# Who issues 32 stores: from SyncE's DMA queue to ScalarE's

## The chip, the cores and the metric

The kernel runs on one core of one Trainium2 chip. TensorE (PE) multiplies matrices, VectorE (DVE), ScalarE (ACT) and GpSimd (POOL) work elementwise, SyncE (SP) computes nothing and issues the DMA transfers. The metric is device time in microseconds (us) for one execution; the figure for a kernel is the median of its runs. Beside the runs one execution was recorded by the hardware profiler; its page and its trace are the source of every other number.

## The reference

The inputs are `x` (8 batches, 8 heads, 512 tokens, 64 features) and `state` (8, 8, 32, 64). For each batch and head two attentions are computed, and their results stand behind each other along the tokens:

```
scores = scale * x @ state^T;   xread = softmax(scores) @ state     # 512 rows
scores2 = scale * state @ x^T;  sread = softmax(scores2) @ x        # 32 rows
```

The heads are joined to rows of 512 features (8 x 544 rows), and a feed-forward layer with a rational function follows, with `w_in` 512 x 2048 and `w_out` 2048 x 512 given in 64-bit floating point:

```
h = rows @ w_in
P = a0 + a1*h + a2*h^2 + a3*h^3
Q = 1 + |b0|*|h| + |b1|*h^2
out = (P / (Q + 1e-6)) @ w_out
```

## The kernel before, in words

The kernel never forms xread. Since xread @ w_in = softmax @ (state @ w_in), it computes the product of state and w_in once for each batch, called m here, and multiplies the transposed attention weights with it. The work of the feed-forward layer is cut into steps n = 8 * batch + u, where u counts eight slices of 256 columns of w_in; eight more steps at the end (n = 64 to 71) handle the sread rows of all batches.

**The order.** Every engine executes its instructions in program order. That order is written out by hand in `ORDER` as a list of tokens; the loop at the end of `attention_rational_ffn` calls one function for each token under a manual schedule. An instruction waits for the semaphores of what it depends on, and whatever stands behind it on the same engine waits too. This holds for SP's queue as well: a DMA whose data isn't ready holds back the DMAs behind it.

**The early stage** (to about 145 us) does these things at once:

- The 64-bit weights are loaded into `raw` tiles (L277 for w_in, L285 for w_out) and turned into 32-bit values: one ACT instruction (`conv_parts`, L300) and several on DVE (`join_rest` L309, `join_low` L321, `join_sign` L332). A finished slice of w_in is used at once and is also stored to HBM (L336). The w_out slices are split into a high and a low part by ACT (L342) and POOL (L343).
- Token `X:i` (`extra`, L626): PE multiplies the states of two batches with slice u of w_in, for all eight slices and four pairs of batches, so 32 times. The result fills a PSUM tile `ps_x` from the pool `ps_h`, tag `h`; this tag has two buffers, which the `h` tiles of the steps and several attention tiles share.
- Token `XA:i` (`extra_out`): ACT copies the tile from PSUM to an SBUF tile `xo` (L638; two buffers), and a DMA stores it to `m32` in HBM (L639). For the pair with batches 0 and 1 only batch 1 is copied and stored (8 stores of 256 KB); the other 24 are of 512 KB. Batch 0's part is used directly from PSUM (`fold_hi0`, L650 on ACT, and `fold_lo0`, L654 on DVE).
- Attention and the steps of batch 0 run beside this.

**A step** consists of the matmuls `F` (L705, into `h`), then on ACT the two functions C (L717) and A (L724), on DVE the products (L728, L732, L738), on ACT the absolute value (L744), logarithm and exponential for the reciprocal (L811, L821), on DVE L749, L755, L761, on POOL L768, and then the matmuls with w_out (L777), which accumulate into PSUM tiles `o`.

**The late stage** (from about 145 us) is these steps for the other batches. Their m is loaded back from `m32` (`load_m`, L660) into tiles that share the `raw` buffers, and split by ACT (L665) and POOL (L666).

All DMAs of the kernel are issued by SP: loads of the raw weights, of xT (L366) and x (L374) for the attention, the stores of w_in (L336) and of m (L639), the reloads of m (L660) and w_in (L349), and the stores of the output (L801, L804).

Of the kernel before, what the change touches and what calls it, by code (L numbers as in the profile page):

```python
# [186 lines left out]
def attention_rational_ffn(  # L187
# [6 lines left out]
    nc = tc.nc  # L194
# [439 lines left out]
    def extra_out(i, copy):  # L634
        u, e = divmod(i, B // 2)
        q0 = 1 if e == 0 else 0
        t = ew.tile([P, 2, 2, CW], F32, name="xo", tag="xo", bufs=2)
        copy(t[:, :, q0:], XP[i][:, :, q0:])  # L638
        nc.sync.dma_start(  # L639
            m32[2 * e + q0 : 2 * e + 2, u].rearrange("q p j f -> p j q f"),  # L640
            t[:, :, q0:],
        )
# [188 lines left out]
    def keep_warm(k):  # L831
# [38 lines left out]
        "lw": load_win,  # L870
        "X": extra,
        "XA": lambda i: extra_out(i, nc.scalar.copy),
        "XV": lambda i: extra_out(i, nc.vector.tensor_copy),
        "lm": load_m,
        "ls": load_state,
# [61 lines left out]
```

## Time and profile before

| | value |
|---|---|
| median of 3 runs | 718.27 us |
| lowest and highest of them | 716.25 and 720.06 us |
| profiled execution: its own time | 720.89 us |
| profiled execution: span from first to last instruction | 719.1 us |
| granted TensorE clock, mean over the span | 0.981 |
| PE busy | 676.1 us (94%) |
| DVE busy | 646.1 us (90%) |
| ACT busy | 516.5 us (72%) |
| POOL busy | 309.0 us (43%) |

The profiled execution lies 2.6 us above the median of the runs. Busy times count computing instructions; issuing a DMA is not counted as busy. In the trace an instruction named SPq is one of SP's sequencer, so a DMA issue. For a DMA the trace has two times: how long the issuing instruction took, and how long after its start the data had landed. The number in brackets behind a line of the timeline is the idle time of the engine before it, with what ended it.

### The profile page before, as it was taken

To read this page: it belongs to the slowest core of one execution; us is meant where nothing else is said; L and a number is where in the kernel's file an instruction comes from. 1 tells how busy PE (TensorE), PEld (TensorE's weight loads), DVE (VectorE), ACT (ScalarE), POOL (GpSimd) and SP (SyncE) were. 2 spreads that over 40 slices of the span, in tenths; PEclk is the share of its full clock that TensorE was granted. 3 is DMA by queue.
4 is the path that set the end of the run, shared out by engine and by line. 5 is a ranking of instruction groups with operands and counts; after the bars stand their busy time and mean duration, and the time that the engine had idled before them with its cause. 6 is when DMAs were issued, how large, how long until landed. Compare 5 with 4: busy or idle time off the path is not lost.

```text
span 719.1 us, 11605 instructions
## 1 busy us (share of the span) xinstructions
PE 676.1 (94%) x4602; PEld 527.7 (73%) x4602; DVE 646.1 (90%) x605; ACT 516.5 (72%) x641; POOL 309.0 (43%) x172
## 2 busy tenths in 40 slices
PE   4578889999999999999999999999999999999994
PEld 3345555677877787778787878787877788888883
DVE  2789998999998999999899999998999889898894
ACT  2678878887777877677587767677787768855752
POOL 0012335385445553463444453535434545534550
PEclk8979999999999999999999999999999999999998
DMA  7988978824030402050313140223041102101201
GB/s 220 318 318 297 342 264 291 269 87 162 16 102 30 147 16 69 35 171 20 103 59 108 40 148 15 61 101 117 1 162 45 59 13 82 38 1 59 89 1 58
DMA packets 47874, 81.49 MB, mean 113 GB/s; under 512 B 3276, under 2 KB 25932, under 8 KB 47820
## 3 DMA queue, kind: packets, MB, share of 16 engines
q1 hardware_dynamic: 47820, 80.75, 33.3%
q8 instruction: 36, 0.59, 0.3%
q14 instruction: 18, 0.15, 0.1%
HBM read 52.95 MB, written 27.79 MB: 112 GB/s over the span
## 4 chain that ended last, share of the span: by engine, by line
PE 74%; DVE 12%; ACT 5%; DMA 4%; issue 2%; POOL 1%; SPq 0%; ACTq 0%; DVEq 0%; POOLq 0%
PE h L705 24%; DMA m_dram<-xo 3%; PE ps_x L626 3%; DVE C L728 2%; DVE A L738 2%; DVE gh L749 2%; PE o__1880 L777 2%; PE o__1823 L777 2%; PE o__3047 L777 2%; DVE C L732 2%; PE o__1899 L777 2%; PE o__3096 L777 2%; PE o__5489 L777 2%; PE o__5507 L777 2%; PE o__5463 L777 2%
## 5 line engine op out<-in xcount | busy, mean ns | idle before, releaser
L768 POOL TENSOR_TENSOR gl<-C,L 128x1024 fp32r<-128x1024 f32 (+1 forms) x71 | 173.8, 2448 | 271.0 <-DVE C L761 209.4
L705 PE MATMUL h<-aT,m 128*128 128x512 f32 x768 | 193.8, 398 | 4.8 <-ACT xo L638 3.7
L705 PEld LDWEIGHTS h<-aT,m 128*128 128x128 f32 x768 | 145.2, 191 | 40.4 <-ACT xo L638 5.1
L749 DVE SCALAR_TENSOR_TENSOR gh<-C,cst,L 128x1024 fp32r<-128x1024 f32 (+1 forms) x72 | 98.7, 1370 | 22.1 <-ACT L L821 3.0
L717 ACT ACTIVATE C<-h,cst 128x1024 f32<-128x1024 f32 (+1 forms) x72 | 83.0, 1155 | 46.7 <-PE h L705 26.2
L666 POOL TENSOR_TENSOR m<-m_sb,m 128x512 fp32r<-128x512 f32 x56 | 82.3, 1473 | 61.5 <-ACT m L665 42.9
L724 ACT ACTIVATE A<-h,cst 128x1024 f32<-128x1024 f32 (+1 forms) x72 | 76.5, 1064 | 44.4 <-PE h L705 41.3
L744 ACT ACTIVATE A<-A 128x1024 f32<-128x1024 f32 (+1 forms) x72 | 72.7, 1012 | 34.2 <-DVE A L738 34.2
L761 DVE SCALAR_TENSOR_TENSOR C<-C,cst,A 128x1024 f32<-128x1024 f32 (+1 forms) x72 | 93.2, 1294 | 1.7
L738 DVE SCALAR_TENSOR_TENSOR A<-A,b0a,h 128x1024 f32<-128x1024 f32 (+1 forms) x72 | 87.1, 1211 | 6.0 <-ACT C L717 5.6
L728 DVE TENSOR_TENSOR C<-C,h 128x1024 f32<-128x1024 f32 (+1 forms) x72 | 83.0, 1154 | 8.1 <-ACT C L717 6.1
L755 DVE SCALAR_TENSOR_TENSOR A<-A,gh 128x1024 f32<-128x1024 f32 (+1 forms) x72 | 88.4, 1228 | 1.6
L732 DVE SCALAR_TENSOR_TENSOR C<-C,cst,h 128x1024 f32<-128x1024 f32 (+1 forms) x72 | 87.8, 1220 | 1.9
L811 ACT ACTIVATE L<-A 128x1024 f32<-128x1024 f32 (+1 forms) x72 | 72.9, 1014 | 8.7 <-POOL gl L768 7.2
L821 ACT ACTIVATE L<-L 128x1024 f32<-128x1024 f32 (+1 forms) x72 | 72.9, 1012 | 0.9
L626 PE MATMUL ps_x<-win_sb,st 64*32 64x256 f32 x1024 | 38.5, 419 | 16.0 <-ACT xo L638 4.9
L343 POOL TENSOR_TENSOR wo<-cv_r,wo 128x512 fp32r<-128x512 f32 x16 | 22.1, 1401 | 61.9 <-ACT wo L342 61.9
L626 PEld LDWEIGHTS ps_x<-win_sb,st 64*32 64x32 f32 x1024 | 18.5, 114 | 31.4 <-ACT xo L638 8.7
L638 ACT COPY xo<-ps_x 128x1024 f32<-128x1024 f32 (+1 forms) x32 | 28.8, 906 | 9.2 <-DMA m_dram<-xo 5.5
L665 ACT CAST m<-m_sb 128x512 fp32r<-128x512 f32 x56 | 33.9, 612 | 1.3 <-PE h L705 1.2
L300 ACT ACTIVATE cv_y<-raw 128x512 f32<-128x512 f32 x32 | 21.3, 685 | 8.0 <-DMA raw<-in_w_in_dram 7.6
L705 PEld LDWEIGHTS h<-sh,m 128*128 128x128 f32 x192 | 24.3, 191 | 1.1 <-issue 0.3
(267 smaller groups left out, 1161.1 us busy)
## 6 DMA issues: line engine op xcount, KB each, us to landing
m_sb<-m_dram SPq DMA_DIRECT2D x56, 256.0 KB, 4.4
m_dram<-xo SPq DMA_DIRECT2D x24, 512.0 KB, 4.4
out_dram<-o_sb SPq DMA_DIRECT2D x34, 256.0 KB, 2.2
xT_sb<-in_xT_dram SPq DMA_DIRECT2D x16, 512.0 KB, 3.9
raw<-in_w_in_dram SPq DMA_DIRECT2D x16, 512.0 KB, 6.1
x_sb<-in_x_dram SPq DMA_DIRECT2D x16, 512.0 KB, 6.0
raw<-in_w_out_dram SPq DMA_DIRECT2D x16, 512.0 KB, 6.4
w_in_dram<-win_sb SPq DMA_DIRECT2D x8, 512.0 KB, 6.4
```

Source lines behind the costliest of these rows:

```text
L626: nc.tensor.matmul(ps[k * NS : (k + 1) * NS, j, q, :], st[j * D : (j + 1) * D, 2 * e + q, k, :], win_t[u][j * D : (j + 1) * D, k, :], star ...
L666: nc.gpsimd.tensor_tensor(m[:, 1], t, m[:, 0].bitcast(F32), op=ALU.subtract)
L705: nc.tensor.matmul(h[:, ci * W : (ci + 1) * W], l, r, start=(q == 0), stop=(q == len(seq) - 1),)
L717: nc.scalar.activation(e["C"], e["h"], AF.Identity, scale=cst[:, 3:4], bias=cst[:, 2:3])
L728: nc.vector.tensor_tensor(e["C"], e["C"], e["h"], op=ALU.mult)
L732: nc.vector.scalar_tensor_tensor(e["C"], e["C"], cst[:, 1:2], e["h"], op0=ALU.add, op1=ALU.mult)
L738: nc.vector.scalar_tensor_tensor(e["A"], e["A"], b0a, e["h"], op0=ALU.add, op1=ALU.mult)
L749: nc.vector.scalar_tensor_tensor(e["gh"], e["C"], cst[:, 0:1], e["L"], op0=ALU.add, op1=ALU.mult)
L755: nc.vector.scalar_tensor_tensor(e["A"], e["A"], 1.0 + 1e-6, e["gh"].bitcast(F32), op0=ALU.add, op1=ALU.mult)
L761: nc.vector.scalar_tensor_tensor(e["C"], e["C"], cst[:, 0:1], e["A"], op0=ALU.add, op1=ALU.subtract)
L768: eng.tensor_tensor(e["gl"], e["C"], e["L"], op=ALU.mult)
L777: nc.tensor.matmul(O[t], e[l][:, j * W + t * P : j * W + (t + 1) * P], wo[:, k, 2 * u + j, :], start=(u == 0 and l == "gh" and k == 0 and ...
```

## The change

The store of `xo` to `m32` is issued by ACT, the engine that has just made the copy, instead of SP. The 32 stores, their tiles, sizes and addresses stay the same, and so does the order of the tokens; no other DMA moves.

```diff
--- before.py
+++ after.py
@@ -636,7 +636,7 @@
         q0 = 1 if e == 0 else 0
         t = ew.tile([P, 2, 2, CW], F32, name="xo", tag="xo", bufs=2)
         copy(t[:, :, q0:], XP[i][:, :, q0:])
-        nc.sync.dma_start(
+        nc.scalar.dma_start(
             m32[2 * e + q0 : 2 * e + 2, u].rearrange("q p j f -> p j q f"),
             t[:, :, q0:],
         )
```

On SP the store was an instruction that waited for the copy's semaphore, with SP's later DMAs behind it. On ACT it is an instruction of ACT's sequencer that waits for the end of the copy on the same engine, with ACT's later instructions behind it.

## The prediction

> **What bounds the kernel now.** I read the stages first: where in the span the 32 stores lie, and which engine is full there. The rows are stretches of the span with the busy time of each engine; the cuts are mine: start-up, the stretch with the stores in three parts, and the rest.
>
> ```profile
> core 0: us, PE busy (x) PEld busy (x) DVE busy (x) ACT busy (x) POOL busy (x), PEclk, DMA share, GB/s
> 17.00:54.00 37.00, 24.27 (x366) 14.81 (x366) 30.67 (x47) 26.71 (x42) 2.53 (x2) 0.82 0.91 314
> 54.00:108.00 54.00, 45.84 (x588) 30.77 (x576) 53.35 (x55) 43.51 (x60) 16.68 (x9) 0.97 0.88 301
> 108.00:145.00 37.00, 35.57 (x490) 23.59 (x489) 33.49 (x38) 32.39 (x44) 17.48 (x10) 1.00 0.82 282
> 145.00:719.10 574.10, 562.32 (x3091) 452.25 (x3090) 524.37 (x462) 409.43 (x490) 271.63 (x146) 1.00 0.20 69
> ```
>
> From 145 us on PE is busy for 562.3 of 574.1 us: PE sets that time, and nothing in it is touched by the change. An early delay can't be won back there: PE has 11.8 us of idle left in the whole of it, and its matmuls follow in program order. So each microsecond by which PE leaves the first 145 us later is nearly a microsecond at the end.
>
> Between 17 and 145 us no engine is the bound alone. DVE is full in the middle (53.4 of 54 us), PE in the last part (35.6 of 37). ACT is busy for 26.7 + 43.5 + 32.4 = 102.6 of 128 us and idle for 25.4. How much of this idle time the stores cost or could take is the question. The next view is that of the tile: the copy, the DMA that stores it, who waited for the copy, and the time from issue to landing.
>
> ```profile
> L638 ACT COPY xo<-ps_x x32: 562/1012/1041, 17.3 to 141.1; 128x1024 f32<-128x1024 f32 x24, 128x512 f32<-128x512 f32 x8
> L639 SPq DMA_DIRECT2D m_dram<-xo x32: 522/585/1198, 18.1 to 142.1; - x32
>   PEld ps_x L626: 8.7, 10
>   PEld h L705: 5.1, 4
> DMA to landing us min/median/max: 2.6/4.5/9.8
> ```
>
> All 32 lie between 17 and 142 us. SP's sequencer spends 0.585 us on an issue (median; 0.522 to 1.198). PE's weight loads waited 14 times, 13.8 us in all, until such a copy had emptied a PSUM buffer: ACT's lateness reaches PE at once, for the two buffers leave no reserve. The last view is the waits between 17 and 145 us: first SP's, then the ACT and DVE waits that the DMAs end.
>
> ```profile
> SPq L639 <- ACT xo L638: 48.4, 19, 5.5
> SPq L639 <- ACT cv_y L300: 9.1, 5, 4.0
> ...
> ACT xo L638 <- DMA m_dram<-xo: 5.5, 6, 1.6
> ACT cv_y L300 <- DMA raw<-in_w_in_dram: 1.6, 2, 1.1
> ...
> DVE cv_r L309 <- DMA raw<-in_w_in_dram: 1.1, 2, 0.6
> ```
>
> SP stands for 57.5 us before stores whose copy isn't made yet. That looks like a great loss, but it is SP's time, and SP computes nothing. What it costs others is in the lower rows: loads of raw weights that came late held ACT for 1.6 us and DVE for 1.1, and a copy that wanted an `xo` buffer whose store hadn't landed held ACT for 5.5 us.
>
> **What the change removes.** From SP it takes 32 issues and 57.5 us of standing. Loads behind a store (L277, L285, L366, L374) can then go out earlier; the most that this can give is the 1.1 + 1.6 us of waits for raw weights. I take 0 for it: the two rows are 4 waits of 1.1 us at most, at the start of the stretch, and later loads wait for buffers that DVE frees. The reloads of m (L660) come late in it and read what was stored long before; POOL's queue is not passed. The transfers stay: the same bytes on the same DMA engines, which are 82 to 91% busy here.
>
> **What it adds.** On ACT, each of the 32 copies is followed by a wait for its own end and by an issue, and all of ACT's next instructions stand behind it. The price is put together from these rows of the timeline and of the chain:
>
> ```profile
> 55.37 9.42 DMA m_dram<-xo
> 64.82 0.04 issue
> 71.30 0.99 ACT L638 COPY xo<-ps_x 128x1024 f32<-128x1024 f32 x1
> 72.19 1.12 ACT L724 ACTIVATE A<-h,cst 128x1024 f32<-128x1024 f32 x1
> 72.32 0.58 SPq L639 DMA_DIRECT2D m_dram<-xo  x1
> ```
>
> Today the next activation starts at 72.19, which is 0.10 us before the copy ends at 72.29: consecutive ones overlap. This overlap goes (0.10). From the copy's end to SP's issue 0.03 us pass; the issue takes 0.585; from a released wait to the next instruction I take the chain's 0.04. Together 0.755 us for a large store; for the eight small ones I take the shortest issue, 0.522, and get 0.69. That is 24 * 0.755 + 8 * 0.69 = 23.6 us of ACT's time. No row shows an issue on ACT. The nearest row is the same transfer issued by SP, and I take that. The bounds are the longest issue of such a store, 1.198 us, and SP's shortest issue of any kind:
>
> ```profile
> 14.12 0.23 SPq L237 DMA_DIRECT2D cst<-in_cb_dram  x1
> ```
>
> With 0.23 us a store costs 0.40 us, 12.8 us in all; with 1.198 it costs 1.37, 44 us in all.
>
> The Trainium skill, page "DMA: Bandwidth & Descriptors", section "Issuing engines are not separate DMA queues", speaks against the change: whoever issues, the transfers share the 16 DMA engines, and issuing elsewhere saves only the sequencer's time for starting them. By that rule the gain is SP's 32 issues, which nobody waits for, and the sum stays what ACT pays.
>
> **How much of it reaches the end.** 23.6 us of new work against 25.4 us of idle time: by the total ACT could just hold it; by parts it can't. At 0.755 and 0.69 us, the 8 stores up to 54 us cost 5.8 us (idle 10.3), the 14 up to 108 us 10.4 (idle 10.5), the 10 after that 7.4 (idle 4.6, so 2.8 too much even if every gap were used). Gaps are used only where they lie. So I walked along the chain that ended last and looked, at each place where ACT stands on it, how many stores come before it and how much idle time lies between them. The rows are ACT's own, with the idle time in brackets, and three pieces of the chain (77.48, 82.47, 102.49):
>
> ```profile
> 28.40 1.93 ACT L638 COPY xo<-ps_x 128x1024 f32<-128x1024 f32 x2
> 33.77 1.01 ACT L638 COPY xo<-ps_x 128x1024 f32<-128x1024 f32 x1 [1.00 <-DMA m_dram<-xo]
> 51.78 0.59 ACT L638 COPY xo<-ps_x 128x512 f32<-128x512 f32 x1
> 58.00 0.62 ACT L638 COPY xo<-ps_x 128x512 f32<-128x512 f32 x1
> 64.86 1.01 ACT L638 COPY xo<-ps_x 128x1024 f32<-128x1024 f32 x1 [1.59 <-DMA m_dram<-xo]
> 67.17 1.02 ACT L638 COPY xo<-ps_x 128x1024 f32<-128x1024 f32 x1 [0.70 <-ACT cv_y L300]
> 69.01 0.27 ACT L585 COPY srT<-ps_sr__472 128x128 f32<-128x128 f32 x1 [0.82 <-PE ps_sr__472 L580]
> 75.31 1.03 ACT L638 COPY xo<-ps_x 128x1024 f32<-128x1024 f32 x1
> 77.48 0.56 ACT cv_y L300
> 82.47 0.70 ACT cv_y L300
> 101.26 0.56 ACT L638 COPY xo<-ps_x 128x512 f32<-128x512 f32 x1
> 101.72 0.58 ACT L650 CAST m<-ps_x 128x512 fp32r<-128x512 f32 x1
> 102.49 0.61 DVE m L654
> 119.09 0.58 ACT L638 COPY xo<-ps_x 128x512 f32<-128x512 f32 x1 [1.19 <-DMA m_dram<-xo]
> 121.10 2.18 ACT L638 COPY xo<-ps_x 128x1024 f32<-128x1024 f32 x2
> 134.86 1.93 ACT L638 COPY xo<-ps_x 128x1024 f32<-128x1024 f32 x2 [0.83 <-PE ps_x L626]
> 139.90 0.99 ACT L638 COPY xo<-ps_x 128x1024 f32<-128x1024 f32 x1
> 141.07 1.01 ACT L638 COPY xo<-ps_x 128x1024 f32<-128x1024 f32 x1 [0.17 <-PE ps_x L626]
> 142.14 1.02 ACT L536 CAST aT<-ps_a 128x1024 fp32r<-128x1024 f32 x1
> ```
>
> - At 33.77 two stores stand before the copy, 1.51 us, and a gap of 1.00 takes up most: +0.5.
> - At 64.86 three (after 51.78, 54.17 and 58.00), 2.14 us, gap 1.59: +0.55.
> - At 77.48 four (after 64.86, 67.17, 71.30, 75.31), 3.02 us, gaps 0.70 and 0.82: +1.5.
> - At 82.47 the store of the copy just ended comes in between, without a gap: +0.75.
> - At 102.49 DVE needs ACT's cast, which ends at 102.30; with the small store ahead of it 102.99: +0.5.
> - At 121.10 and behind it the small store and one large one, 1.45 us; the gap of 1.19 before them is used up by the two stores ahead of it: +1.4.
> - At 142.14 the stores after the two copies at 134.86 and the one at 139.90, 2.27 us, with 0.17 of gap: +2.1. Here PE, full until then, needs the PSUM buffer and the cast.
>
> The sum is +7.3 us. Elsewhere longer gaps lie behind the stores; I count nothing there. That cover is thin where ACT's gap is a wait for PE and PE in turn waits for ACT's copies: then the gap moves along with the delay and takes up nothing.
>
> Against the profiled execution this gives 720.9 + 7.3 = 728.2 us; that execution is 2.6 us above the median of the runs, so I forecast 718.3 + 7.3 = **725.6 us**. With the cheapest issue (0.40 us a store) the same walk gives 0, 0, 0.1, 0.4, 0.2, 0.4 and 1.0: +2.1 us, or 720.4. With twice the walk, that is, if a delay also eats the gaps behind it, it is +14.6, or 732.9. These two are the forecast's own range.
>
> **Rivals.** The first ends on the other side: *faster, because stores no longer stand in SP's line.* Today a store is queued behind loads that SP issued before it, and the landing spreads from 2.6 to 9.8 us; ACT's wait for it is 5.5 us. If on its own queue a store lands near the short end, this 5.5 goes, and with the raw loads' 2.7 at most 8.2 us are won. It decides if ACT's issue costs near the lower bound: then -5.5 + 2.1 = -3.4, or 714.9 us. For it speaks that the wait for a store stands in the walk at 33.77, 64.86 and 119.09; against it, that these gaps are the very ones that take up the issues in my sum, and that ACT is then free only to stand at the issue. The Trainium skill, page "DMA: Bandwidth & Descriptors", section "Queues, rings and completion order", supports this rival: a DMA engine alternates between the queue rows that have work. No run shows it yet; the only dynamic queue of this kernel is SP's.
>
> The second: *no change.* ACT's 25.4 us of idle time hold the 23.6 us, since PE's and DVE's waits are elastic at those places: 718.3 us. For it speaks the total; against it, the last 37 us, where ACT lacks 2.8 us, and DVE, which has 0.65 us of reserve in the middle.
>
> The third: *the whole price.* ACT becomes the bound, each gap moves along, and all 23.6 us show: 741.9 us. For it speak ACT's 54 us between 54 and 108, which would be full to 53.9; against it, the gaps up to 54 us, which wait for DVE and for raw loads and hold 5.8 us easily.
>
> That the change doesn't do what it says I rule out: one call names the issuing engine, and nothing else depends on it.
>
> **How the numbers follow.** The forecast gets 0.61, the whole price 0.11, no change 0.18, faster 0.10. A measurement here can tell about 0.5% from no change, 3.6 us. Of the forecast's 0.61, 0.06 lies under +3.6 us. So slower is 0.55 + 0.11 = 0.66, same 0.18 + 0.06 = 0.24, faster 0.10. The range goes from 716 us, into the faster case, to 737 us, beyond twice the walk; it leaves out part of the faster case and most of the whole price, under 2 in 10 together.
>
> **What would show it.** In the profile of the changed kernel, 32 issues at L639 should stand on ACT's queue at about 0.585 us, each followed by a gap of some 0.65 us before ACT's next instruction; SP's waits at L639 should be gone. PE's idle time between 17 and 145 us, now 22.3 us, should be some 7 us more, and the stretch behind it as long as before. The sum is wrong if ACT's instructions overlap the issue (no gap behind the copy), if an issue on ACT is far from 0.585 us, or if the late stretch changes length. The faster rival is right if ACT's wait for stores vanishes and landings shorten without PE's idle time growing.

## The result: slower by 2.7%, and the profile after

The median went from 717.8 us (of four runs; the table ahead of the prediction has three) to 739.0 us: the ratio is 1.0268, with a 95% interval of 1.023 to 1.0306, so 19.2 us over the kernel before by the ratio (21.2 between the medians). The direction was forecast, the size was not: the forecast was +7.3 us, and the range ended at 737. The profiled execution took 738.26 us, its span is 736.5, which is 17.4 more than the span of before; that pair is compared here.

The first view cuts each span at the same instruction, the start of PE's matmuls into `h` that stood at 142.1 us before (157.7 us after). The columns are those of the stretches in the prediction. The kernel before:

```profile
17.00:142.10 125.10, 102.81 (x1416) 66.85 (x1416) 115.26 (x136) 100.04 (x141) 33.80 (x20) 0.93 0.87 299
142.10:719.10 577.00, 565.19 (x3103) 454.56 (x3102) 526.62 (x464) 412.01 (x494) 274.53 (x147) 1.00 0.21 70
```

The changed kernel:

```profile
17.00:157.70 140.70, 106.60 (x1417) 68.63 (x1414) 114.52 (x135) 100.68 (x140) 35.56 (x20) 0.90 0.80 269
157.70:736.50 578.80, 566.41 (x3102) 455.71 (x3102) 527.12 (x463) 412.11 (x494) 271.92 (x147) 0.99 0.21 69
```

15.6 of the 17.4 us are lost in the early stretch, 1.8 behind it. In the early one PE's idle time grows from 125.1 - 102.8 = 22.3 to 140.7 - 106.6 = 34.1 us, so by 11.8; the other 3.8 us are PE's own: the same matmuls took longer at a granted clock of 0.90 instead of 0.93.

The next rows are the tile's in the changed kernel, with what its copies waited for, and the timeline of ACT around two copies:

```profile
L639 ACTq DMA_DIRECT2D m_dram<-xo x32: 530/587/612, 17.1 to 157.7; - x32
  DMA m_dram<-xo: 9.3, 6
DMA to landing us min/median/max: 3.3/4.9/10.8
```

```profile
27.70 1.01 ACT L638 COPY xo<-ps_x 128x1024 f32<-128x1024 f32 x1
28.74 0.59 ACTq L639 DMA_DIRECT2D m_dram<-xo  x1
31.31 1.01 ACT L638 COPY xo<-ps_x 128x1024 f32<-128x1024 f32 x1 [2.61 <-DMA m_dram<-xo]
32.35 0.59 ACTq L639 DMA_DIRECT2D m_dram<-xo  x1
32.98 0.59 ACT L536 CAST aT<-ps_a__295 128x512 fp32r<-128x512 f32 x1 [0.66 <-ACT xo L638]
```

The reader sees two losses. One is what was priced: the copy ends at 32.32, the issue starts 0.03 later, takes 0.59, and ACT's next instruction begins 0.66 us after the copy's end. The other wasn't in the sum: the copy at 31.31 first stands 2.61 us until a store has landed and freed its `xo` buffer. Before, ACT's copies stood 5.5 us for landings; now it is 9.3, and one more wait of 1.9 us that the view puts down to DVE belongs to it, so 11.2 us in all; for in the chain it is a landing that ends it:

```profile
88.64 10.67 DMA m_dram<-xo
99.35 0.04 issue
99.39 0.59 ACT xo L638
```

### The profile page after: what moved, and what is told of

The parts are those of the page before. It is cut to its first block, busy times and chain, and to the rows that moved or that the text cites. A ratio compares the mean times of both kernels' runs of the same rounds, so it can differ in the third digit from the quotient of the medians.

```text
span 736.5 us, 11591 instructions
## 1 busy us (share of the span) xinstructions
PE 681.1 (92%) x4602; PEld 530.9 (72%) x4602; DVE 646.6 (88%) x605; ACT 518.0 (70%) x641; POOL 308.2 (42%) x172
## 4 chain that ended last, share of the span: by engine, by line
PE 65%; DVE 14%; ACT 7%; DMA 7%; issue 3%; POOL 1%; ACTq 1%; SPq 0%; DVEq 0%; POOLq 0%
PE h L705 22%; DMA m_dram<-xo 5%; DVE gh L749 2%; ACT xo L638 2%; DVE C L728 2%; DVE A L738 2%; DVE C L761 2%; DVE A L755 2%; PE ps_x L626 2%; DVE C L732 2%; PE o__5489 L777 2%; PE o__5507 L777 2%; PE o__6031 L777 2%; PE o__4314 L777 2%; PE o__6046 L777 2%
## 5 line engine op out<-in xcount | busy, mean ns | idle before, releaser
L705 PE MATMUL h<-aT,m 128*128 128x512 f32 x768 | 196.0, 401 | 6.0 <-ACT xo L638 4.1
L705 PEld LDWEIGHTS h<-aT,m 128*128 128x128 f32 x768 | 146.8, 193 | 42.5 <-ACT xo L638 5.8
L666 POOL TENSOR_TENSOR m<-m_sb,m 128x512 fp32r<-128x512 f32 x56 | 80.8, 1447 | 62.4 <-ACT m L665 43.9
L626 PE MATMUL ps_x<-win_sb,st 64*32 64x256 f32 x1024 | 40.3, 435 | 24.6 <-ACT xo L638 12.5
L300 ACT ACTIVATE cv_y<-raw 128x512 f32<-128x512 f32 x32 | 21.2, 680 | 11.1 <-DMA raw<-in_w_in_dram 7.0
```

What stands on the lines that cost most here:

```text
L626: nc.tensor.matmul(ps[k * NS : (k + 1) * NS, j, q, :], st[j * D : (j + 1) * D, 2 * e + q, k, :], win_t[u][j * D : (j + 1) * D, k, :], star ...
L666: nc.gpsimd.tensor_tensor(m[:, 1], t, m[:, 0].bitcast(F32), op=ALU.subtract)
L705: nc.tensor.matmul(h[:, ci * W : (ci + 1) * W], l, r, start=(q == 0), stop=(q == len(seq) - 1),)
```

## The experiments

Two theories stood against each other. Theory 1: ACT's standing behind each copy, and the gaps that move along with it. Theory 2: stores that land late and keep the two buffers. The median of before differed from job to job (717.8 to 722.0 us); so each kernel is given as a ratio to the runs of before on its own chip.

**The issue alone.** The stores stay on SP, and ACT issues something small beside each, read from the same tile.

```diff
+        nc.scalar.dma_start(
+            m32[0, u, 16 * e : 16 * e + 16],
+            t[16 * e : 16 * e + 16, :, 1],
+        )
```

> The kernel before, its stores on SP as they were, and beside each one an additional small DMA issued by ACT (32 KB, a part of the same xo tile into a part of m32 that nobody reads): the issue and its wait on ACT without the moved transfer. Theory 1: if the small DMA's issue takes ACT 0.4 to 0.6 us, the time is 717.8 + 12 to 20 = 730 to 738 us. Theory 2: the stores still land as before and SP is held as before, so at most 722 us.

Measured: 1.0105 (1.0079 to 1.013), +7.6 us. Though it carries 32 KB, the issue takes ACT nearly as long as that of a store of 512 KB, and the gap is the same:

```profile
L643 ACTq DMA_DIRECT2D m_dram<-xo x32: 555/564/645, 16.8 to 149.2; - x32
```

```profile
46.80 1.02 ACT L638 COPY xo<-ps_x 128x1024 f32<-128x1024 f32 x1
47.84 0.56 ACTq L643 DMA_DIRECT2D m_dram<-xo  x1
48.45 1.06 ACT L815 ACTIVATE L<-A 128x1024 f32<-128x1024 f32 x1 [0.64 <-ACT xo L638]
```

It fell between the two: below theory 1's 730 us by the ratio, above theory 2's 722. Its copies stood only 1.3 us for landings, so the 7.6 us are the price of ACT's standing, and about 12 us of the change are something else. The stretch of PE shows it as well: up to the same `h` 132.2 us, of which 102.4 busy, so 29.8 us idle, 7.5 more than before, and no loss of clock.

```profile
17.00:149.20 132.20, 102.42 (x1413) 66.81 (x1412) 114.76 (x135) 100.39 (x139) 35.50 (x20) 0.94 0.86 288
```

Two more doses: a shorter issue (a single row),

```diff
+        nc.scalar.dma_start(
+            m32[0, u, 16 * e : 16 * e + 1, 0],
+            t[16 * e : 16 * e + 1, 0, 1],
+        )
```

> The kernel before, stores on SP, and beside each a DMA of one row (1 KB) issued by ACT, so that ACT's issue is as short as one can be here (0.23 us was SP's shortest). Dose below the 0.56 us of the first such run, which cost 1.05%. If ACT's standing counts by its length as in the prediction's walk (gaps take up the first part of it), 0.2 to 0.35 us an issue give 2 to 4 us: 1.003 to 1.006 of before. If each stop costs the same whatever its length (the wait for the copy's end and the restart), it stays near 1.01.

and two issues one behind the other:

```diff
+        for w in (0, 64):
+            nc.scalar.dma_start(
+                m32[0, u, 16 * e + w : 16 * e + w + 16],
+                t[16 * e : 16 * e + 16, :, 1],
+            )
```

> The same with two small DMAs (32 KB each) issued by ACT one behind the other: about 1.2 us of standing behind each copy, 19 us more than with one. If the first dose had used up the gaps, the second shows almost in full: 1.0105 plus 14 to 19 us, 1.030 to 1.037 of before. If half of it is still taken up, 1.020 to 1.026.

Measured: 1.0047 (1.003 to 1.0064) for an issue of 0.20 us and a gap of 0.28, and 1.0399 (1.0371 to 1.0426) for two issues. The rows are of the short one (all its issues, then one issue and what follows it) and of the double one:

```profile
L643 ACTq DMA_DIRECT2D m_dram<-xo x32: 200/201/464, 18.6 to 146.1; - x32
```

```profile
50.16 0.20 ACTq L643 DMA_DIRECT2D m_dram<-xo  x1
50.40 1.06 ACT L815 ACTIVATE L<-A 128x1024 f32<-128x1024 f32 x1 [0.28 <-ACT xo L638]
```

```profile
52.07 1.31 ACTq L644 DMA_DIRECT2D m_dram<-xo  x2
53.43 1.06 ACT L816 ACTIVATE L<-A 128x1024 f32<-128x1024 f32 x1 [1.39 <-issue]
```

So the price goes with the length of the standing: 3.4, 7.6 and 28.7 us for gaps of 0.28, 0.64 and about 1.4 us, where 32 gaps and lost overlaps come to 12, 24 and 48 us. The short issue came out within its forecast; the double one missed its own (1.030 to 1.037) on the far side. A third of the standing shows at first; from the first full dose to the second 21 of 24 us show. But these 21 us aren't all idle time. The early stretch of the double one, up to the same `h`:

```profile
17.00:169.00 152.00, 111.25 (x1417) 70.59 (x1417) 116.73 (x137) 100.89 (x141) 35.28 (x20) 0.86 0.80 261
```

Against the run with one issue PE is idle for 152.0 - 111.25 = 40.75 instead of 29.8 us, so 11 us more; the same matmuls take 8.8 us longer, at a granted clock of 0.86 instead of 0.94. So ACT's idle time takes up about two thirds of the first issue and still some half of the second; the rest of the second one's price is the lower clock.

**Three buffers for xo.** This takes nearly all waits for landings away in both kernels.

```diff
-        t = ew.tile([P, 2, 2, CW], F32, name="xo", tag="xo", bufs=2)
+        t = ew.tile([P, 2, 2, CW], F32, name="xo", tag="xo", bufs=3)
...
-    srT = cp.tile([P, NP, B * NS], F32, name="srT")
+    srT = cp.tile([P, NP, NS], F32, name="srT")
```

> The changed kernel with three xo buffers instead of two. To make room, srT keeps one batch's sread only (each batch overwrites the one before, and the last eight steps use the last one for all batches: that part of the output is left out) and the row of ones shares a tile. Theory 1: ACT's gaps behind the copies stay, the buffer waits of 11.2 us go but were partly cover for the issues: 730 to 736 us. Theory 2: the waits for xo were the cause, so the time falls to 718 to 724 us.

> The control: the kernel before with three xo buffers and the same part of the output left out. Both theories: ACT's 5.5 us of waits for xo go, at most 5.5 us are won, so 712 to 718 us; the effect of three buffers on the changed kernel is read against this one.

Measured: the changed kernel 1.0118 (1.0088 to 1.0149), the kernel before 0.9979 (0.9963 to 0.9995). Of the changed kernel's 11.2 us of waits for landings one of 3.0 us is left (the view puts it down to DVE; by the semaphores in the trace it is a landing), and it gets 1.5% faster; the kernel before gains 0.2%. The waits for buffers are therefore worth some 9 us in the changed kernel (1.5% less 0.2%), and what is left between the two, 1.4% or 10 us, is put down to ACT's standing, of which the issue alone had shown 7.6. Neither range for the changed kernel held: its ratio on the 717.8 us of before is 726 us, between them. The control's did: 716 us. The early stretch of the changed kernel with three buffers shows where the 9 us were:

```profile
17.00:149.00 132.00, 101.94 (x1417) 66.86 (x1417) 116.45 (x137) 101.29 (x142) 35.47 (x20) 0.95 0.84 288
```

With two buffers PE was idle for 34.1 us and busy for 106.6; here it is 30.1 and 101.9, nearly the 29.8 and 102.4 of the issue alone. So of what the late landings cost, 4 us are PE's idle time and 4.7 are matmuls at a lower clock.

**Behind ACT's next instruction.** The stores stay on ACT, but each is issued one instruction later, so that ACT has work meanwhile; first with two buffers, then with three.

```diff
-        nc.scalar.dma_start(
-            m32[2 * e + q0 : 2 * e + 2, u].rearrange("q p j f -> p j q f"),
-            t[:, :, q0:],
-        )
+        late.append(
+            lambda: nc.scalar.dma_start(
+                m32[2 * e + q0 : 2 * e + 2, u].rearrange("q p j f -> p j q f"),
+                t[:, :, q0:],
+            )
+        )
...
         for name, args in tokens:
+            behind = len(late)
             ops[name](*args)
+            if name in (...):
+                for _ in range(behind):
+                    late.pop(0)()
```

(The list holds the tokens that give ACT work in the early stage.)

> The changed kernel, but each of the 32 stores is issued on ACT behind ACT's next instruction instead of right behind the copy, so that ACT already has work while its sequencer waits for the copy and issues. Theory 1 (ACT's standing: about 0.76 us per store, which reaches the end nearly in full because ACT's gaps move along with the delay): the gap of 0.66 us behind each copy goes, and the time falls from 739.0 to about 718 to 723 us. Theory 2 (landing: on its own queue, beside loads that SP now issues earlier, a store lands late, and the copies wait for xo buffers, 11.2 us where it was 5.5): the stores go out no earlier, so the time stays above 730 us.

> Both causes taken away at once: the stores on ACT behind ACT's next instruction, and three xo buffers (with the part of the output left out that srT's cut costs). If ACT's standing and the waits for xo are the whole of the loss, the time is that of the kernel before with three buffers, 0.998 of before, within 3 us: 714 to 720 us on a chip where before has 717.8. If something else is in it (SP's order of loads), it stays above 724 us.

Measured: 1.0201 (1.0164 to 1.0237) with two buffers, 1.0006 (0.9989 to 1.0024) with three. With two the first theory's forecast fell and the second's, above 730 us, held (732 us by the ratio). The timeline of the run with two buffers shows why:

```profile
38.92 0.58 ACT L639 COPY xo<-ps_x 128x512 f32<-128x512 f32 x1 [0.30 <-DMA m_dram<-xo]
38.94 0.59 ACTq L641 DMA_DIRECT2D m_dram<-xo  x1
44.20 1.12 ACT L727 ACTIVATE A<-h,cst 128x1024 f32<-128x1024 f32 x1 [4.70 <-PE h L708]
44.26 0.53 ACTq L641 DMA_DIRECT2D m_dram<-xo  x1
...
52.54 1.00 ACT L639 COPY xo<-ps_x 128x1024 f32<-128x1024 f32 x1
53.43 1.07 ACT L814 ACTIVATE L<-A 128x1024 f32<-128x1024 f32 x1
53.57 0.59 ACTq L641 DMA_DIRECT2D m_dram<-xo  x1
54.39 0.68 ACT L300 ACTIVATE cv_y<-raw 128x512 f32<-128x512 f32 x1
```

At 53.57 it works as meant: the issue lies inside the activation of 53.43 to 54.50, and the next one starts at 54.39, with no gap. But the copy that ended at 39.50 is stored at 44.26 only, since the activation ahead of the store waited for PE until 44.20, and the store waited with it. Late stores keep buffers: the copies stood 16.8 us for landings. With three buffers one such wait of 2.9 us is left (the copy at 36.26 takes the buffer whose store went out at 28.72 and landed 7.5 us later), and the loss is gone: both causes together are the whole of it, to within 0.3% of the kernel before with three buffers. From 1.0118 to 1.0006 it is 1.1% or 8 us that go with ACT's standing, near the 7.6 of the issue alone.

**Why the stores land late.** Theory A: SP no longer stands at the stores, so its loads go out earlier and share the transfers with them. Theory B: the stores' own queue takes turns by packets, and its packets of 1 KB are small. The first is tried by a small store on SP at the old place,

```diff
+        nc.sync.dma_start(
+            m32[0, u, 16 * e : 16 * e + 16],
+            t[16 * e : 16 * e + 16, :, 1],
+        )
```

> The changed kernel (stores on ACT) with a small store of 32 KB on SP at the old place, read from the same xo tile into a part of m32 that nobody reads: SP again waits for each copy before it issues the loads behind. The first runs put about 7 us of the 21 to ACT's standing and the rest to stores that land late. Theory A (the landing suffers because SP's loads are no longer held and crowd the transfers): the copies' waits for xo buffers fall from 11.2 us to about 5 and the time to about 726 to 731 us. Theory B (the landing suffers because the stores have a queue of their own, whose 1 KB packets take turns with the larger ones of the loads, so that loads issued later overtake a store): the time stays at 734 to 740 us.

the second by another layout of the tile:

```diff
-        copy(t[:, :, q0:], XP[i][:, :, q0:])
+        copy(t[:, q0:].rearrange("p q j f -> p j q f"), XP[i][:, :, q0:])
...
-            m32[2 * e + q0 : 2 * e + 2, u].rearrange("q p j f -> p j q f"),
-            t[:, :, q0:],
+            m32[2 * e + q0 : 2 * e + 2, u].rearrange("q p j f -> p q (j f)"),
+            t[:, q0:].rearrange("p q j f -> p q (j f)"),
```

> The changed kernel with the xo tile laid out as batch, half, column, so that a store's contiguous runs are 2 KB instead of 1 KB, on both sides. Theory B: half as many packets per store and twice the bytes per turn, so the stores land sooner, the waits for xo fall from 11.2 us to about 5, and the time to 727 to 733 us. Theory A: the packets' size changes nothing that matters, 735 to 740 us.

Measured: with SP held 1.0144 (1.0119 to 1.017), with packets of 2 KB 1.0167 (1.0144 to 1.019). The waits tell the two apart, first SP held, then 2 KB with its issue:

```profile
ACT xo L638 <- DMA m_dram<-xo: 3.4, 2, 2.2
```

```profile
L639 ACTq DMA_DIRECT2D m_dram<-xo x32: 338/366/376, 16.9 to 154.3; - x32
  DMA m_dram<-xo: 12.7, 8
```

Holding SP took the waits from 11.2 to 3.4 us and 1.2% of the time, to 728 us by the ratio, which is what theory A said; the stores still had their own queue. Larger packets came to 730 us, in theory B's range and not in theory A's, but left the waits at 12.7 us, so theory B's reason fell. Where the gain of 1.0% comes from stays open. The issue is shorter, 0.366 instead of 0.587 us, but PE's idle time up to the same `h` is the same, 137.3 - 103.0 = 34.3 us against 34.1; what is less in the profiled pair is PE's own time, at a clock of 0.93 instead of 0.90:

```profile
17.00:154.30 137.30, 103.05 (x1414) 67.43 (x1413) 114.60 (x135) 100.58 (x139) 34.89 (x20) 0.93 0.79 276
```

One store and the loads around it are an example of theory A. SP in the changed kernel, whose store of 88.64 took 10.7 us to land by the chain above:

```profile
88.45 1.34 SPq L374 DMA_DIRECT2D x_sb<-in_x_dram  x2
90.38 1.62 SPq L285 DMA_DIRECT2D raw<-in_w_out_dram  x2
```

With SP held, the same store went out at 86.06, and the same loads 1.7 us behind it instead of 0.2 us ahead (the small store is at L643); it landed in 5.4 us:

```profile
86.05 1.64 SPq L643 DMA_DIRECT2D m_dram<-xo  x1
87.78 1.86 SPq L374 DMA_DIRECT2D x_sb<-in_x_dram  x2
89.73 0.86 SPq L285 DMA_DIRECT2D raw<-in_w_out_dram  x2
```

The median landing says little (4.5 us before, 4.9 after): what counts is which store meets which loads, and whether a copy then wants its buffer.

Then both at once, the 2 KB layout and SP held, and the 2 KB layout on the kernel before (the diffs are the ones above; the small store reads the same rows in the new layout).

> The changed kernel with the 2 KB layout and with SP held by a small store at the old place. So far: issue on ACT alone +1.05% (issue of 0.56 us), SP held takes the changed kernel from +2.7% to +1.4%, the 2 KB layout shortens ACT's issue from 0.587 to 0.366 us and takes it to +1.7% although the waits for xo stay (12.7 us). If the loss is the sum of ACT's standing and of the waits that SP's unheld loads cause, each part comes off by itself: 1.0145 minus about 32 * 0.22 = 7 us at most, so 1.005 to 1.010 of before. If the two fixes overlap (both only move the same waits), it stays at 1.012 or more.

> The kernel before with the 2 KB layout of xo, stores on SP: SP's issue gets shorter, which nobody waits for, and a store has half as many packets. If the packets' size limits the transfers in this stage, the 5.5 us of waits for xo shrink and 1 to 4 us are won (0.995 to 0.999 of before); if not, the time is that of before (0.998 to 1.002). Either way it is the candidate for a kernel that beats both.

Measured: 1.0134 (1.0114 to 1.0153) and 1.0 (0.9985 to 1.0016). The first missed its forecast of 1.005 to 1.010 and came out where the other branch put it, at 1.012 or more; the issue of a large store was 0.43 us there, not 0.366, and the doses above give about 0.7 to 0.8% for such a gap. Its copies still stood 4.3 us for landings; 0.5% or so stays unexplained. With SP held by a small store at 1.0144, against 1.0105 for the issue alone, the same kind of rest is seen: whether the stores' own queue costs that, or the added small stores, wasn't told apart. On the kernel before the waits fell from 5.5 to 2.7 us, and nothing was won. Nothing found here beats the kernel before beyond its uncertainty, except three buffers, which leave out part of the output.

**POOL as the issuer.**

```diff
-        nc.sync.dma_start(
+        nc.gpsimd.dma_start(
```

> The stores issued by POOL instead of SP or ACT: ACT pays nothing, SP is not held, and the stores have a queue of their own. If late landing counts by itself (A or B), the time is 717.8 + about 10 = 726 to 732 us; if only ACT's standing counted, 716 to 721 us. POOL's own share: it is idle for most of the first 145 us, and its issues may take it longer than 0.6 us each.

Measured: 1.0513 (1.0474 to 1.0551), far beyond both forecasts. POOL has the idle time, but the stores go out late, and the copies stood 41.6 us for landings, 15 times, up to 6.7 us. The rows are three large stores, one behind the other, then, from the chain, the landing of the first, and from the view of the tile for the second store alone, its time to landing:

```profile
86.66 0.93 POOL L639 DMA_DIRECT2D m_dram<-xo  x1 [0.80 <-ACT L L821]
91.77 0.92 POOL L639 DMA_DIRECT2D m_dram<-xo  x1 [4.19 <-issue]
101.36 0.93 POOL L639 DMA_DIRECT2D m_dram<-xo  x1 [8.68 <-issue]
```

```profile
86.66 4.80 DMA m_dram<-xo
DMA to landing us min/median/max: 9.3/9.3/9.3
```

The first landed at 86.66 + 4.8 = 91.46, and the second goes out 0.3 us later; that one landed at 101.06, and the third goes out 0.3 us later, though its copy had ended at 92.57 and POOL stood idle. It is so for all 16 large stores that follow a large one: none is issued before that one has landed. A small store next to a large one doesn't wait like this. What holds the large ones back wasn't tried. The run doesn't separate the theories, since each of its issues takes 0.92 us and comes late.

## Why the prediction was wrong, point by point

**The price of an issue was right.** 0.03 + 0.585 + 0.04 us of gap were put together from SP's rows; the gap is 0.66 us, the issue 0.587.

**How much of it reaches the end was right, for this part.** The walk along the chain gave +7.3 us; the issue alone, measured by itself, cost 7.6. The places hold too: the walk sums to 3.3, 3.8, 5.2 and 7.3 us at the last four steps, and the starts of PE's matmuls in that run lag behind those of before by 1.5, 2.1, 4.6 and 7.1 (the run had come out of the start-up 0.9 us earlier). The last step names the cast at 142.14 too; PE's `h` started at 142.13, ahead of it, so what it needed was the copy. In the changed kernel itself PE's idle time grew by 11.8 us and not by the 7 that the forecast said.

**The step that failed is in "What the change removes".** It says of SP's loads that they "can then go out earlier; the most that this can give is the 1.1 + 1.6 us", and takes 0. It bounded this edit from above and not from below: an earlier load was allowed to be a gain or nothing. It was a loss of about 9 us, as large as ACT's own. SP's standing (57.5 us in the two rows shown, 64.9 with the smaller ones at L639) wasn't idle; it kept the loads behind the stores while the DMA engines were 82 to 91% busy, and with two buffers a landing that comes late stops ACT, then PE. Experiments: SP held, -1.2%; three buffers, -1.5%. Nor did the sum have a term for PE's clock: about half of the 9 us are matmuls that took longer.

**The faster rival had the sign of this reversed.** It expected the 5.5 us of waits to go once stores left SP's line. They became 11.2.

**The whole price came near the number for another reason.** 741.9 us were worked out as 23.6 us of standing shown in full. Only a third of that shows; the rest of the way is the waits, with the slower matmuls that came with them, and some 0.4% that stayed open.

**The late stretch was right to 0.3%**: 577.0 us before, 578.8 after; nothing was won back.

## What to carry to other kernels

A queue that stands in order before a store also paces the loads behind it; when such a wait is removed, ask what is let loose, and price it as a loss as well as a gain wherever transfers are near full and buffers are two. Issuing a DMA right behind the instruction that makes its data stops that engine for the wait, the issue and the restart; one instruction later it costs next to nothing (0.3% here), if a further buffer bears the later start. What an engine with idle time can take up is found by doses: the first one here showed to a third, the second almost whole, half of it as PE's idle time and the rest as a lower clock.

## What the hardware showed that was not expected

- The length of an issue hardly goes with its bytes: 0.587 us for 512 KB and 0.564 for 32 KB in pieces of 1 KB, 0.366 for 512 KB in pieces of 2 KB (0.43 where SP was held too), 0.20 for a single piece of 1 KB. On POOL's queue the store took 0.92 us.
- A DMA issue behind an activation that waits starts only when that activation starts (44.26 behind 44.20, with the data ready since 39.50). All 32 issues of that run start 0.01 to 0.16 us after the start of the instruction ahead of them: here ACT's sequencer doesn't go past a waiting instruction.
- In the changed kernel PE's matmuls were slower: the granted clock in the early stretch was 0.93 before, 0.90 after, and over the whole span PE was busy for 681.1 us instead of 676.1 with the same 4602 matmuls. The amount of idle time alone doesn't say it: 29.8 us of it went with 0.94 (the issue alone), 34.3 with 0.93 (the 2 KB layout), 34.1 with 0.90 (the changed kernel), 40.8 with 0.86 (two issues). What sets it wasn't tried.
- On POOL's queue a large store behind a large one went out only 0.3 us or more after that one had landed, 16 times of 16.
